# Making w_out the stationary operand of the MLP's second product, with sums in one PSUM tile per expert tile and earlier fetches for the first two experts

## The chip, the cores and the metric

The kernel runs on one core of one Trainium2 chip. The metric is the device time of one execution in microseconds (us). The kernel before was run three times: 5398.34, 5403.23 and 5403.87 us, median 5403.23. One further execution was profiled; it took 5409.9 us, of which the recorded span covers 5408.1 us, so 1.8 us lie outside the span.

## The reference, cut to what matters

Three stages on x of 8 x 3072 tokens with 256 features, all in float32.

```
scores = z @ z.T / S                     # z: 8 x 3072 x 64
x      = u * (relu(scores)**2 @ v)       # attention; u, v: 8 x 3072 x 256

e      = argmax(normalized(x) @ normalized(emb).T / tau)        # one of 8 experts
x      = gate * (relu(x @ w1[e]) @ w2[e])                       # 256 -> 1024 -> 256

h      = x @ w_in                                               # 256 -> 2048
x      = where(h > 0, h, exp(min(h, 0)) - 1) @ w_out            # 2048 -> 256
```

## The kernel before, in words

Matrix operands are split into a high and a low part, and a product is the sum of three: high by high, high by low, low by high. Each TensorE matmul has a stationary operand of 128x128 (loaded ahead of it) and a moving one of up to 512 columns, and adds to a PSUM tile.

The program is one list of 1166 steps. Step n issues on TensorE the first product of its own step (`h`, into a tile `pss`, two buffers) and the second product of the step two before (`acc`, into a tile `psa`, two buffers); between them ScalarE (ACT) and VectorE (DVE) make the hidden values and their high and low parts. The first 576 steps are attention: 48 chunks of 512 tokens, 12 steps each. Then come the units of the MoE and the MLP, laid out by a list: A is an expert's tile of 512 tokens (4 steps), B the 256-token remainder of an expert (2 steps), M the MLP on the tokens of an A (8 steps) and D the MLP on 512 remainder rows (8 steps). There are 41 A, 21 B, 41 M and 7 D. The first ones are A0 at step 576, A1 at 580, M0 at 584, A2 at 592, M1 at 596, A3 at 604, M2 at 608, A4 at 616; D0 begins at 1110 and the last, D6, at 1158. D6 has functions of its own (`l_h`, `l_acc`); `m_acc` is the second product of the 41 M and of the other six D, 47 units of 8 steps.

In `m_acc` the hidden values are stationary, 128 tokens at a time, and w_out moves: 8 matmuls of 512 columns (a high and a low half of w_out side by side) and 8 of 256 columns per step. The four token quarters stand in two PSUM tiles, `psa`, with the two sums (`wh` and `wl`) in 512 columns. In the last step of a unit ACT copies them out in four pieces (`o`, `o2`, line 1057 and 1058), and one step later `m_out` adds the two on DVE and scatters four blocks of 128 rows to the output with indirect DMAs.

Attention's second product is laid out the other way: v is stationary, the hidden values move, and the sums stand in one `psa` tile, features on partitions. `evac_ops` turns such a tile in 32x32 blocks on DVE (`tr`), writes it to DRAM in four pieces (`put`) and reads it back as rows (`get`).

Work beside the products is laid into steps: `at` puts it after step n's own instructions, `spread` and `pairs` deal it over a stretch of steps by given costs. Every engine and each of the two DMA queues (SP and POOL) works in the order of the program. POOL carries the indirect DMAs: scatters of token numbers by expert into `tok` (line 573, `sc` of `route_ops`; each waits until the one before it has landed), gathers of token numbers (`ids`), of token rows (`rows`) and of an expert's weights (`wst`) on line 779, and scatters of result rows to `out` on line 784. The tokens are routed in 24 groups, of which the first 22 end in attention; the last two are laid into the units. Each group has eight scatters of token numbers. `rows` are then put to DRAM (`xg`) and read back in the blocked layout by SP.

At the start `zero_dram` fills `tok` and the last four chunks of `xs` with zeros through SP. `slot` gives out SBUF from a ring of 48 tiles that all kinds share, in order of the program: an operation waits until the readers of what its slot held before are done.

Of the kernel before, what the change touches and what calls it, by code (L numbers as in the profile page):

```python
# [16 lines left out]
LAG = 2  # L17
# [10 lines left out]
def attn_moe_mlp(ctx, tc, zT, u, v, emb, tau, wp, w_in, w_out, out):  # L28
# [26 lines left out]
    xg = dr.tile([(NA + NB) * 512, D], F32, name="xg")  # L55
    tok = dr.tile([E * N, 1], I32, name="tok")
# [161 lines left out]
    def zero_dram():  # L218
# [6 lines left out]
        for C in range(NCH - 4, NCH):  # L225
            sp.dma_start(xs[C * 512:(C + 1) * 512, :].rearrange("(t p) d -> p t d", p=128),
                         zt.bitcast(F32).rearrange("p (t d) -> p t d", t=4))
# [171 lines left out]
    def att_acc(C, m):  # L399

        if m == 0:
            AC[C] = t_acc()
        hi, lo = HL.pop((C, m))
        vt = V[C // NC, m]
        for part in range(2):
            for dc in range(2):
                a = AC[C][:, dc]
                for j in range(2):
                    vh, vl = (vt[:, j, o + dc * 128:o + dc * 128 + 128] for o in (0, 256))
                    if part == 0:  # L410
                        mm(a, vh, hi[:, j], m == 0 == j, False)
                        mm(a, vl, hi[:, j], False, False)
                    else:
                        mm(a, vh, lo[:, j], False, m == CS - 1 and j == 1)

    def evac_ops(C):

        g, o = chunk_group[C]
        h = {}
        rows = xr[C * 512:(C + 1) * 512, :]  # L420

        def tr():
            h["t"] = slot("xt", F32, (16, 2, 32))
            vec.transpose(out=h["t"], in_=AC.pop(C).rearrange("p a (b r) -> p b a r", r=32))
# [6 lines left out]
        def get():  # L431
            X[C] = slot("x", F32, (4, 256))
            sp.dma_start(X[C], rows.rearrange("(t p) d -> p t d", p=128))
# [383 lines left out]
    def rows_ops(key):  # L817
# [9 lines left out]
        def gi(t):  # L827
            def fn():
                if t == 0:
                    IDS[key] = sb.tile([128, 4], I32, name="ids", tag="ids", bufs=6)  # L830
# [105 lines left out]
    PR = set()  # L936

# [44 lines left out]
    def l_acc(key, i):  # L982
# [15 lines left out]
        if last:  # L998
            if hf == 0:
                PS[key] = slot("o", F32, (4, 256)), None  # L1000
            o = PS[key][0][:, 2 * hf:2 * hf + 2]
            cp(o, a[:, :, 256:])
            tt(o, o, a[:, :, :256], ALU.add)
            for fn in m_out(key)[1 + 2 * hf:3 + 2 * hf]:
                fn()
# [28 lines left out]
    def m_acc(key, i):  # L1034
        if i == 0:
            AC[key] = [t_acc(), t_acc()]
        hi, lo = HL.pop((key, i))
        w = WO[i]
        last = i == NF2 // 2 - 1
        for qs in ((0, 1), (2, 3)) if last else ((0, 1, 2, 3),):  # L1040
            for part in range(2):
                for q in qs:
                    a = AC[key][q // 2][:, q % 2]
# [368 lines left out]
```

## Time and profile before

| | |
|---|---|
| median of three runs | 5403.23 us (5398.34 to 5403.87) |
| profiled execution | 5409.9 us |
| its span | 5408.1 us |
| mean granted TensorE clock | 0.996 |
| TensorE busy | 5363.7 us (99%) |
| VectorE busy | 4245.2 us (78%) |
| ScalarE busy | 4086.1 us (76%) |
| POOL busy | 1393.0 us (26%) |

The share of an engine is its busy time over the span. A busy TensorE includes matmuls that run at a lower granted clock and the modelled ends of matmuls, so the distance between starts tells more than the busy time: 512 columns at the full clock start 227 ns apart. In the rows of a timeline, consecutive instructions of one kind are joined (x8), the first number is the start, the second the time to the end of the last; the bracket holds the idle time before the instruction and what ended it.

### The profile page before, as it was taken

What the parts mean: (1) busy time and instruction counts of PE and PEld (TensorE: products, weight loads), DVE (VectorE), ACT (ScalarE), POOL (GpSimd) and SP (SyncE); (2) the same over time, 40 slices, a digit from 0 to 9 for tenths busy, and PEclk for the clock granted to TensorE, in tenths of its full rate; (3) what the DMA queues carried; (4) which work ended last, traced back from release to release, by engine and by line L of the source; (5) the groups of instructions that cost most, each with busy time, mean ns of one, the idle gap of its engine ahead of it and who ended that gap; (6) DMA issues with size and microseconds to landing.
All of it is one profiled execution on the core that took longest, in us unless ns stands there. A gap on an engine that the chain in (4) does not pass through costs nothing. (4 is left out here: it accounts for less than half of the span.)

```text
span 5408.1 us, 73322 instructions
## 1 busy us (share of the span) xinstructions
PE 5363.7 (99%) x26064; PEld 4531.1 (84%) x26064; DVE 4245.2 (78%) x7905; ACT 4086.1 (76%) x4764; POOL 1393.0 (26%) x1205
## 2 busy tenths in 40 slices
PE   9999999999999999999999999999999999999998
PEld 7888888888888887888888888888888888888887
DVE  8888888888888887887777777777777777777887
ACT  7989988898899985666666666666666666666786
POOL 0011101011111104323444444344544122231011
PEclk9999999999999999999999999999999999999999
DMA  3333333232323325112332323232323122221110
GB/s 111 86 79 86 79 86 84 73 90 75 86 81 76 83 58 178 57 52 87 92 100 86 103 89 98 88 106 89 100 84 110 45 68 67 67 67 36 20 24 20
DMA packets 465743, 428.17 MB, mean 79 GB/s; under 512 B 276380, under 2 KB 407199, under 8 KB 465376
## 3 DMA queue, kind: packets, MB, share of 16 engines
q1 hardware_dynamic: 388480, 216.86, 15.2%
q0 software_dynamic: 76896, 206.62, 12.2%
q8 instruction: 206, 3.38, 0.3%
q14 instruction: 161, 1.32, 0.1%
HBM read 293.72 MB, written 119.40 MB: 76 GB/s over the span
## 5 line engine op out<-in xcount | busy, mean ns | idle before, releaser
L104 PE MATMUL psa<-hi,v 128*128 128x512 f32 x4608 | 1143.8, 390 | 2.7 <-DVE hi L387 2.7
L104 PEld LDWEIGHTS psa<-hi,v 128*128 128x128 f32 x4608 | 865.1, 188 | 182.6 <-DVE hi L387 3.9
L83 DVE TENSOR_TENSOR lo<-r,hi 128x1024 fp32r<-128x1024 f32 x576 | 705.7, 1225 | 243.7 <-ACT hi L101 238.5
L104 PE MATMUL pss<-x2h,wi 128*128 128x512 f32 x2624 | 814.1, 391 | 0.0
L104 PE MATMUL psa<-wo,hi 128*128 128x512 f32 x3072 | 775.6, 390 | 0.6 <-DVE hi L1025 0.6
L366 ACT ACTIVATE r<-pss 128x1024 f32<-128x1024 f32 x576 | 591.2, 1026 | 208.4 <-PE pss L104 205.3
L93 DVE SCALAR_TENSOR_TENSOR y<-e,y 128x1024 f32<-128x1024 f32 x384 | 467.6, 1218 | 323.8 <-ACT e L1010 323.6
L957 ACT ACTIVATE e<-pss 128x1024 f32<-128x1024 f32 x376 | 386.5, 1028 | 393.0 <-PE pss L104 389.0
L104 PEld LDWEIGHTS psa<-wo,hi 128*128 128x128 f32 x3072 | 574.0, 188 | 117.4 <-DVE hi L1025 0.9
L371 ACT ACTIVATE r<-r 128x1024 f32<-128x1024 f32 x576 | 611.5, 1062 | 18.3
L573 POOL DMA_INDIRECT tok<-idt,pi x192 | 236.6, 1232 | 1505.3 <-DVE pi L552 859.7
L104 PE MATMUL psa<-lo,v 128*128 128x512 f32 x2304 | 616.7, 389 | 0.0
L95 DVE SCALAR_TENSOR_TENSOR junk<-x,en 128x256 f32<-128x256 f32 x1536 | 602.5, 419 | 0.0
L784 POOL DMA_INDIRECT out<-o,ids x192 | 201.8, 1051 | 1551.6 <-DVE o L83 508.3
L884 ACT ACTIVATE hi<-pss 128x1024 fp32r<-128x1024 f32 x206 | 211.8, 1028 | 495.3 <-PE pss L104 430.5
L104 PEld LDWEIGHTS pss<-x2h,wi 128*128 128x128 f32 x2624 | 476.5, 189 | 86.4
L104 PE MATMUL pss<-x2l,wi 128*128 128x512 f32 x1312 | 510.4, 389 | 0.0
L104 PEld LDWEIGHTS psa<-lo,v 128*128 128x128 f32 x2304 | 433.3, 188 | 90.2
L101 ACT ACTIVATE hi<-r 128x1024 fp32r<-128x1024 f32 x462 | 490.5, 1062 | 14.6
L83 DVE TENSOR_TENSOR y<-r,y 128x1024 f32<-128x1024 f32 x384 | 470.6, 1225 | 33.2 <-DVE y L93 0.5
L83 DVE TENSOR_TENSOR lo<-y,hi 128x1024 fp32r<-128x1024 f32 x384 | 470.8, 1226 | 30.5 <-DMA xg<-rows 8.9
L104 PEld LDWEIGHTS psa<-wo,lo 128*128 128x128 f32 x3072 | 429.5, 190 | 41.1 <-DVE lo L83 7.8
(160 smaller groups left out, 9935.7 us busy)
## 6 DMA issues: line engine op xcount, KB each, us to landing
vs<-v SPq DMA_DIRECT2D x48, 512.0 KB, 5.1
u<-u SPq DMA_DIRECT2D x48, 512.0 KB, 5.3
xr<-xt SPq DMA_DIRECT2D x192, 128.0 KB, 2.6
x<-xr SPq DMA_DIRECT2D x48, 512.0 KB, 4.4
xs<-x SPq DMA_DIRECT2D x48, 512.0 KB, 5.0
xg<-rows SPq DMA_DIRECT2D x41, 512.0 KB, 2.9
xt<-xg SPq DMA_DIRECT2D x164, 128.0 KB, 3.0
zz<-zT SPq DMA_DIRECT2D x46, 256.0 KB, 5.3
```

Source lines behind the costliest of these rows:

```text
L83: vec.tensor_tensor(out=o, in0=a, in1=b, op=op)
L93: vec.scalar_tensor_tensor(out=o, in0=a, scalar=s, in1=b, op0=op0, op1=op1)
L95: vec.scalar_tensor_tensor(out=o, in0=a, scalar=s, in1=b, op0=op0, op1=op1, accum_out=acc)
L101: act.activation(out=o, in_=a, func=AF.Copy)
L104: pe.matmul(o, lhsT=l, rhs=r, start=start, stop=stop, skip_group_check=True)
L366: act.activation(out=r, in_=p, func=AF.Relu, scale=1.0 / S)
L371: act.activation(out=r, in_=r, func=AF.Square)
L573: pool.indirect_dma_start(out=tok[:, :], out_offset=bass.IndirectOffsetOnAxis(ap=h["pi"][:, t:t + 1], axis=0), in_=K["idt"][:, gt:gt + 1], ...
L784: pool.indirect_dma_start(out=dst, out_offset=bass.IndirectOffsetOnAxis(ap=idx, axis=0), in_=src, in_offset=None, bounds_check=bound, oob_ ...
L884: act.activation(out=hi, in_=p, func=AF.Relu)
L957: act.activation(out=e, in_=p, func=AF.Relu, scale=-1.0)
```

## The change

Four edits.

1. The MLP's second product takes the layout of attention's: `vw_acc`, cut out of `att_acc`, serves both. w_out is stationary, the hidden values move: 12 matmuls of 512 columns per step into one `psa` tile. In the last step of a unit `out_ops` turns the tile on DVE, then SP writes it to a new DRAM tile `orow` in four pieces and reads it back as rows, and four scatters to the output follow at steps n+13 and n+14 of a unit that began at n. The ACT copies and the DVE addition of the 47 units go. The columns of w_out come permuted from the host, and `l_acc` of the last unit puts its features back in order as it copies, one quarter at a time.
2. The eight scatters of token numbers of a group are laid one a step, from the step on in which all eight stood.
3. The rows of A0 are gathered from step 556 on (before: 563), its weights from 560 (567); the rows of A1 from 562 (567).
4. `zero_dram` fills eight chunks of `xs` instead of four. The `ids` tiles get eight buffers instead of six.

The core of the diff:

```diff
@@ -53,6 +53,7 @@
+    orow = dr.tile([N, D], F32, name="orow")
...
@@ -222,7 +223,7 @@
             sp.dma_start(tv[a], zt[:, :E * N // 256])
-        for C in range(NCH - 4, NCH):
+        for C in range(NCH - 8, NCH):
             sp.dma_start(xs[C * 512:(C + 1) * 512, :].rearrange("(t p) d -> p t d", p=128),
                          zt.bitcast(F32).rearrange("p (t d) -> p t d", t=4))
...
@@ -396,32 +397,25 @@
-
-        if m == 0:
-            AC[C] = t_acc()
-        hi, lo = HL.pop((C, m))
-        vt = V[C // NC, m]
+    def vw_acc(a, w, hi, lo, first, last):
+
         for part in range(2):
             for dc in range(2):
-                a = AC[C][:, dc]
                 for j in range(2):
-                    vh, vl = (vt[:, j, o + dc * 128:o + dc * 128 + 128] for o in (0, 256))
+                    wh, wl = (w[:, j, o + dc * 128:o + dc * 128 + 128] for o in (0, 256))
                     if part == 0:
-                        mm(a, vh, hi[:, j], m == 0 == j, False)
-                        mm(a, vl, hi[:, j], False, False)
+                        mm(a[:, dc], wh, hi[:, j], first and j == 0, False)
+                        mm(a[:, dc], wl, hi[:, j], False, False)
                     else:
-                        mm(a, vh, lo[:, j], False, m == CS - 1 and j == 1)
-
-    def evac_ops(C):
-
-        g, o = chunk_group[C]
+                        mm(a[:, dc], wh, lo[:, j], False, last and j == 1)
+
+    def rows_by_dram(rows, acc, get_tile):
+
         h = {}
-        rows = xr[C * 512:(C + 1) * 512, :]
         def tr():
             h["t"] = slot("xt", F32, (16, 2, 32))
-            vec.transpose(out=h["t"], in_=AC.pop(C).rearrange("p a (b r) -> p b a r", r=32))
+            vec.transpose(out=h["t"], in_=acc().rearrange("p a (b r) -> p b a r", r=32))
         def put():
             for i in range(4):
@@ -429,8 +423,21 @@
                              h["t"][i * 32:(i + 1) * 32].rearrange("p b a c -> p b (a c)"))
         def get():
+            sp.dma_start(get_tile(), rows.rearrange("(t p) d -> p t d", p=128))
+        return tr, put, get
+
+    def att_acc(C, m):
+        if m == 0:
+            AC[C] = t_acc()
+        vw_acc(AC[C], V[C // NC, m], *HL.pop((C, m)), m == 0, m == CS - 1)
+
+    def evac_ops(C):
+
+        g, o = chunk_group[C]
+        def x_tile():
             X[C] = slot("x", F32, (4, 256))
-            sp.dma_start(X[C], rows.rearrange("(t p) d -> p t d", p=128))
+            return X[C]
+        tr, put, get = rows_by_dram(xr[C * 512:(C + 1) * 512, :], lambda: AC.pop(C), x_tile)
         def mul():
             if o == 0:
...
@@ -827,7 +834,7 @@
-                    IDS[key] = sb.tile([128, 4], I32, name="ids", tag="ids", bufs=6)
+                    IDS[key] = sb.tile([128, 4], I32, name="ids", tag="ids", bufs=8)
...
@@ -997,12 +1005,13 @@
         if last:
             if hf == 0:
-                PS[key] = slot("o", F32, (4, 256)), None
-            o = PS[key][0][:, 2 * hf:2 * hf + 2]
-            cp(o, a[:, :, 256:])
-            tt(o, o, a[:, :, :256], ALU.add)
-            for fn in m_out(key)[1 + 2 * hf:3 + 2 * hf]:
-                fn()
+                PS[key] = slot("o", F32, (4, 256))
+            for q in range(2):
+                o = PS[key][:, 2 * hf + q]
+                ov = o.rearrange("p (i b c) -> p b i c", i=4, b=2)
+                cp(ov, a[:, q, 256:].rearrange("p (b i c) -> p b i c", i=4, b=2))
+                tt(ov, ov, a[:, q, :256].rearrange("p (b i c) -> p b i c", i=4, b=2), ALU.add)
+                scatter(out[:, :], o, IDS[key][:, 2 * hf + q:2 * hf + q + 1], N - 1)
     def m_g(key, i):
         p, e, y = PS[key, i]
...
@@ -1033,48 +1042,31 @@
     def m_acc(key, i):
         if i == 0:
-            AC[key] = [t_acc(), t_acc()]
-        hi, lo = HL.pop((key, i))
-        w = WO[i]
-        last = i == NF2 // 2 - 1
-        for qs in ((0, 1), (2, 3)) if last else ((0, 1, 2, 3),):
-            for part in range(2):
-                for q in qs:
-                    a = AC[key][q // 2][:, q % 2]
-                    sl = slice(q * 128, q * 128 + 128)
-                    for j in range(2):
-                        st = last and j == 1
-                        if part == 0:
-                            mm(a, hi[:, j, sl], w[:, j], i == 0 and j == 0, st)
-                        else:
-                            mm(a[:, :256], lo[:, j, sl], w[:, j, :256], False, st)
-            if last:
-                q = qs[1]
-                if q == 1:
-                    PS[key] = slot("o", F32, (4, 256)), slot("o2", F32, (4, 256))
-                o, t = PS[key]
-                ap = AC[key][q // 2]
-                cp(t[:, q - 1:q + 1], ap[:, :, 256:])
-                cp(o[:, q - 1:q + 1], ap[:, :, :256])
-
-    def m_out(key):
-        def add():
-            o, t = PS[key]
-            tt(o, o, t, ALU.add)
+            AC[key] = t_acc()
+        vw_acc(AC[key], WO[i], *HL.pop((key, i)), i == 0, i == NF2 // 2 - 1)
+
+    def out_ops(key):
+
+        i = OUTS.setdefault(key, len(OUTS))
+        h = {}
+
+        def tile_():
+            h["o"] = slot("o", F32, (4, 256))
+            return h["o"]
         def sc(q):
             def fn():
                 ids = IDS["A", key[1]] if key[0] == "M" else IDS[key]
-                scatter(out[:, :], PS[key][0][:, q], ids[:, q:q + 1], N - 1)
-            return fn
-        return [add] + [sc(q) for q in range(4)]
+                scatter(out[:, :], h["o"][:, q], ids[:, q:q + 1], N - 1)
+            return fn
+        return rows_by_dram(orow[i * 512:(i + 1) * 512, :], lambda: AC.pop(key), tile_) + tuple(sc(q) for q in range(4))
     def d_prep(key):
         h = {}
         def ld():
             h["t"] = slot("xt", F32, (16, 2, 32))
-            IDS[key] = sb.tile([128, 4], I32, name="ids", tag="ids", bufs=6)
+            IDS[key] = sb.tile([128, 4], I32, name="ids", tag="ids", bufs=8)
             j = key[1]
             rows = dn[j * 512:(j + 1) * 512, :].rearrange("(b r) (a i c) -> i r b a c", r=32, a=2, i=4)
             for i in range(4):
...
@@ -1278,8 +1270,8 @@
         w += L
-        for s_ in sc:
-            at(w, s_, 1)
+        for i, s_ in enumerate(sc):
+            at(w + i, s_, 1)
         spread(gs, w, w + L, 0.2)
         route_end[g] = w
...
@@ -1314,12 +1306,15 @@
             wr = max(n - 9, lo_)
+            if un == units[0]:
+                w, wr = n - 16, n - 20
+                assert wr >= lo_
             if pv is not None and pv[0] == "B" == k:
                 assert False
             if pv is not None and pv[0] == "M" and prev[pv] is not None and prev[pv][0] in "AB":
                 wr = max(n - 16, lo_)
-            elif k == "A" and un[1] < 2:
-                wr = max(n - 13, lo_)
+            elif un == units[1]:
+                wr = n - 18
             for o in ro:
                 at(wr, o, 2)
             for o in wl:
...
@@ -1348,8 +1343,12 @@
             spread([tr], n - 4, n - 3, 1.25)
             pre[n - 2] += hl
         if k in "MD" and un != units[-1]:
-            w = n + nst[k] + LAG + (2 if k == "D" else 0)
-            spread(m_out(un), w, w + 2)
+            w = n + nst[k] + LAG - 1
+            tr, put, get, *sc = out_ops(un)
+            at(w, tr)
+            at(w + 1, put)
+            at(w + 2, get)
+            spread(sc, w + 4, w + 6)
     def emit(n, k):
         if 0 <= n < len(steps):
...
@@ -1380,8 +1379,7 @@
-    B, S, _ = v.shape
-    vp = v.reshape(B, S, 4, 2, 32).transpose(0, 1, 3, 2, 4).reshape(B, S, D)
+    vp, op = (t.reshape(-1, 4, 2, 32).transpose(0, 2, 1, 3).reshape(t.shape) for t in (v, w_out))
@@ -1390,7 +1388,7 @@
-        "w_in": c(w_in).view(np.int64), "w_out": c(w_out).view(np.int64),
+        "w_in": c(w_in).view(np.int64), "w_out": c(op).view(np.int64),
```

POOL's indirect DMAs around A0, in the kernel before: `zq<-zp` closes attention's own part, `tok` are the scatters of token numbers of group 21, `ids`, `rows` and `wst` the gathers of A0, of A1 and the ids of A2.

```order
L325 DMA zq<-zp 64x1024
L326 DMA zq<-zp 64x1024
L573 DMA tok<-idt,pi 196608x1 x8
L779 DMA ids<-tok,ixa 128x1 x4
L779 DMA rows<-xs,ids 128x256 x4
L779 DMA wst<-wp,wia 128x1024 x4
L779 DMA ids<-tok,ixa 128x1 x4
L779 DMA rows<-xs,ids 128x256 x4
L779 DMA wst<-wp,wia 128x1024 x4
```

The same place in the changed kernel, whose lines are numbered differently:

```order
L326 DMA zq<-zp 64x1024
L327 DMA zq<-zp 64x1024
L786 DMA ids<-tok,ixa 128x1 x4
L786 DMA rows<-xs,ids 128x256 x4
L580 DMA tok<-idt,pi 196608x1
L786 DMA wst<-wp,wia 128x1024 x4
L580 DMA tok<-idt,pi 196608x1 x2
L786 DMA ids<-tok,ixa 128x1 x4
L786 DMA rows<-xs,ids 128x256 x4
```

A0's ids and rows stand ahead of all eight scatters, its weights behind one of them, A1's ids and rows behind three; five more follow.

POOL's DMAs a little later, in the kernel before, from the conversion of the MLP's weights (`wi`, `wo`) on: the gathers behind the eight scatters are A3's.

```order
L1147 DMA wi<-wis 128x1024 x8
L1153 DMA wo<-wos 128x1024 x8
L779 DMA wst<-wp,wia 128x1024 x4
L573 DMA tok<-idt,pi 196608x1 x8
L779 DMA ids<-tok,ixa 128x1 x4
L779 DMA rows<-xs,ids 128x256 x4
```

And in the changed kernel:

```order
L1139 DMA wi<-wis 128x1024 x8
L1145 DMA wo<-wos 128x1024 x8
L786 DMA wst<-wp,wia 128x1024 x4
L580 DMA tok<-idt,pi 196608x1 x5
L786 DMA ids<-tok,ixa 128x1 x4
L786 DMA rows<-xs,ids 128x256 x4
L580 DMA tok<-idt,pi 196608x1 x3
L786 DMA wst<-wp,wia 128x1024 x4
```

A3's gathers stand behind five scatters instead of eight; the last three come after them.

DVE at the end of M0 (step 593) in the changed kernel: `lo<-pss,hi` belongs to an A step, `w<-wst,w` splits weights, `junk,dot<-x,en` are the dot products of the routing.

```order
L84 TENSOR_TENSOR y<-r,y 128x1024
L1034 CAST hi<-y 128x1024
L84 TENSOR_TENSOR lo<-y,hi 128x1024
L94 SCALAR_TENSOR_TENSOR lo<-pss,hi 128x1024
L84 TENSOR_TENSOR w<-wst,w 128x512 x3
L418 STREAM_TRANSPOSE xt<-psa 128x1024
```

Before, the same rows stand there without the last one; the addition `o<-o,o` of M0 came later, between the dot products of the next step. The turning of the PSUM tile is new at this place, with the dot products of the step behind it.

## Rows read from the trace of the kernel before

**Rows 1.** The page: busy time, share of the span and instructions of each engine.
```profile
PE 5363.7 (99%) x26064; PEld 4531.1 (84%) x26064; DVE 4245.2 (78%) x7905; ACT 4086.1 (76%) x4764; POOL 1393.0 (26%) x1205
```

**Rows 2.** Timeline of PE in one MLP step: start, us, engine, line, operation, tiles.
```profile
2334.00 0.63 PE L104 MATMUL pss<-x2h,wi 128*128 128x512 f32 x2
...
2336.75 1.98 PE L104 MATMUL psa<-wo,hi 128*128 128x512 f32 x8
2338.56 1.12 PE L104 MATMUL psa<-wo,lo 128*128 128x256 f32 x8
2339.51 0.63 PE L104 MATMUL pss<-xh,w 128*128 128x512 f32 x2
```

**Rows 3.** Timeline of PE: an expert step (two starts), and sixteen MLP steps.
```profile
2224.06 0.61 PE L104 MATMUL pss<-xh,w 128*128 128x512 f32 x2
2229.50 0.61 PE L104 MATMUL pss<-x2h,wi 128*128 128x512 f32 x2
...
5250.90 0.63 PE L104 MATMUL pss<-xh,wi 128*128 128x512 f32 x2
5339.18 0.40 PE L104 MATMUL pss<-xh,wi 128*128 128x256 f32 x2
```

**Rows 4.** Timeline of PE: the step starts on either side of three stalls.
```profile
2080.32 0.39 PE L104 MATMUL pss<-zp 128*128 128x512 f32 x1
2104.60 0.39 PE L104 MATMUL pss<-zp 128*128 128x512 f32 x1
...
2205.92 0.63 PE L104 MATMUL pss<-xh,w 128*128 128x512 f32 x2
...
2345.03 0.63 PE L104 MATMUL pss<-xh,w 128*128 128x512 f32 x2
2364.83 0.62 PE L104 MATMUL pss<-xh,w 128*128 128x512 f32 x2
```

**Rows 5.** Busy times in the first stall: stretch, then PE, PEld, DVE, ACT, POOL, PEclk, DMA.
```profile
2080.00:2104.00 24.00, 14.78 (x49) 11.05 (x48) 11.62 (x24) 14.04 (x21) 16.15 (x15) 0.72 0.70 210
```

**Rows 6.** Timelines of ACT and DVE: the three waits behind the stalls.
```profile
2085.87 0.63 ACT L101 ACTIVATE w<-wst 128x512 fp32r<-128x512 f32 x1 [8.48 <-DMA wst<-wp,wia]
...
2213.45 1.02 ACT L884 ACTIVATE hi<-pss 128x1024 fp32r<-128x1024 f32 x1 [11.48 <-DMA xg<-rows]
...
2353.43 1.23 DVE L83 TENSOR_TENSOR lo<-y,hi 128x1024 fp32r<-128x1024 f32 x1 [8.88 <-DMA xg<-rows]
```

**Rows 7.** Timeline of POOL: first scatter of eight, and first gather behind them, three times.
```profile
2032.34 1.05 POOL L573 DMA_INDIRECT tok<-idt,pi  x1 [49.92 <-DVE pi L552]
...
2068.97 1.10 POOL L779 DMA_INDIRECT ids<-tok,ixa  x1 [2.70 <-DMA tok<-idt,pi]
...
2156.27 1.14 POOL L573 DMA_INDIRECT tok<-idt,pi  x1 [0.30 <-DVE junk L95]
...
2197.18 1.04 POOL L779 DMA_INDIRECT ids<-tok,ixa  x1 [3.02 <-DMA tok<-idt,pi]
...
2302.22 1.63 POOL L573 DMA_INDIRECT tok<-idt,pi  x1 [0.30 <-issue]
...
2336.64 1.95 POOL L779 DMA_INDIRECT ids<-tok,ixa  x1 [2.39 <-DMA tok<-idt,pi]
```

**Rows 8.** Groups by line, engine and tile: busy us, mean ns, idle before.
```profile
L424 DVE STREAM_TRANSPOSE xt<-psa 128x1024 f32<-128x1024 f32 x48 | 60.0, 1249 | 81.3 <-PE psa L104 81.3
```

**Rows 9.** Timelines of ACT and DVE at the end of an MLP unit.
```profile
5172.46 1.09 ACT L101 ACTIVATE o<-psa 128x512 f32<-128x512 f32 x2 [0.35 <-PE psa L104]
5177.02 1.23 DVE L93 SCALAR_TENSOR_TENSOR y<-e,y 128x1024 f32<-128x1024 f32 x1 [3.59 <-ACT e L1010]
```

**Rows 10.** Timelines of SP's queue and ACT at the start.
```profile
9.72 6.79 SPq L226 DMA_DIRECT2D xs<-zt  x4
26.81 0.62 ACT L101 ACTIVATE v<-vs 128x512 fp32r<-128x512 f32 x1
```

**Rows 11.** The page, DMA issues: KB each and median us from issue to landing.
```profile
x<-xr SPq DMA_DIRECT2D x48, 512.0 KB, 4.4
```

More of the change, by code (lines that the diff above doesn't have):

```diff
@@ L397, in att_lo @@
         HL[C, m] = [hi, lo]
-    def att_acc(C, m):
-        if m == 0:
-            AC[C] = t_acc()
-        hi, lo = HL.pop((C, m))
-        vt = V[C // NC, m]
+    def vw_acc(a, w, hi, lo, first, last):
         for part in range(2):
             for dc in range(2):
-                a = AC[C][:, dc]
                 for j in range(2):
-                    vh, vl = (vt[:, j, o + dc * 128:o + dc * 128 + 128] for o in (0, 256))
+                    wh, wl = (w[:, j, o + dc * 128:o + dc * 128 + 128] for o in (0, 256))
                     if part == 0:
-                        mm(a, vh, hi[:, j], m == 0 == j, False)
-                        mm(a, vl, hi[:, j], False, False)
-                    else:
-                        mm(a, vh, lo[:, j], False, m == CS - 1 and j == 1)
-    def evac_ops(C):
-        g, o = chunk_group[C]
+                        mm(a[:, dc], wh, hi[:, j], first and j == 0, False)
+                        mm(a[:, dc], wl, hi[:, j], False, False)
+                    else:
+                        mm(a[:, dc], wh, lo[:, j], False, last and j == 1)
+    def rows_by_dram(rows, acc, get_tile):
         h = {}
-        rows = xr[C * 512:(C + 1) * 512, :]
         def tr():
             h["t"] = slot("xt", F32, (16, 2, 32))
-            vec.transpose(out=h["t"], in_=AC.pop(C).rearrange("p a (b r) -> p b a r", r=32))
+            vec.transpose(out=h["t"], in_=acc().rearrange("p a (b r) -> p b a r", r=32))
         def put():
@@ L936, in attn_moe_mlp @@
     PR = set()
+    OUTS = {}
     def m_r(key, i):
```

## The prediction

> **What bounds the kernel now.** The busy times come first: TensorE is busy 99% of the span, the next engine, VectorE, 78% [rows 1]. So the time falls only where TensorE's own work gets shorter or where it stops waiting, and what the other engines gain or lose counts only once it reaches TensorE. The second view is therefore TensorE's timeline, read from step start to step start. Two things are to be seen in it. The MLP's steps are a little longer than the experts' although both multiply the same number of columns: 2334.00 to 2339.51 is 5.51 us [rows 2], against 5.44 for an expert step, and 88.28 / 16 = 5.52 over sixteen steps of the remainder units [rows 3]. And in the whole program, behind the start, there are three places where it stands still for long [rows 4]. Three attention steps are 48 matmuls of 0.2265 us (eight of 512 columns take 2338.56 - 2336.75 = 1.81 us [rows 2]), 10.9 us; from 2080.32 to 2104.60 they take 24.28, so 13.4 are lost. Two unit steps are 5.51 + 5.44 = 10.95; they take 18.14 from 2205.92 to 2224.06, the latter start in [rows 3], and 19.80 from 2345.03 to 2364.83: 7.2 and 8.85 lost. Together 29.4 us.
>
> The third view, the timelines of ACT and DVE, says what ends these: the landing of A0's weights after 8.48 us of waiting, and twice the landing of `xg`, an expert's rows, after 11.48 and 8.88 us [rows 6]. The fourth, POOL's, says why that data is late: ahead of the gathers stand eight scatters of token numbers, each waiting for the one before it. Eight last 2068.97 - 2032.34 = 36.6 us, 40.9 and 34.4 us: 4.6, 5.1 and 4.3 each [rows 7].
>
> **The second product.** Before, a step of it is 8 matmuls of 512 columns and 8 of 256; now it is 12 of 512, and the number of columns is the same. The eight of 256 take 2339.51 - 2338.56 = 0.95 us, where four of 512 take half of 1.81 = 0.905 [rows 2]. By these starts a step gains 0.045 us. By the length of whole steps it gains more: the new step is made of 24 matmuls of 512 columns, as an expert step is, so it should last 5.44, a gain of 0.07 to 0.077 [rows 2, 3]. I take 0.072, since the whole step is what repeats and the short rows are read from two differences of ends. The steps are 47 units of 8, 376 in all (the last unit keeps its own function): **-27.1 us**, with ends of 0.045 x 376 = 17 and 0.077 x 376 = 29.
>
> The Trainium skill speaks against this, on the page "TensorE: Matmul & The Clock Gate", section "Back-to-back issue gap": an isolated matmul's gap at the full clock is its columns over 2.4 plus 2.5 ns. By that, four matmuls fewer are 10 ns a step, 3.8 us in all, and the sum would come out 23 us higher. This trace differs: 226 ns for 512 columns and 119 for 256 mean about 12 ns that do not shrink with the columns, so the rows set the term, and what the skill's rule would give stands among the rivals.
>
> **What replaces the copies.** At the end of each of the 47 units four ACT copies and a DVE addition go; a DVE turning of the PSUM tile comes, 1.25 us each, as in attention [rows 8]. It waits for TensorE's last matmul of the unit, and behind it in DVE's queue stands the next step's chain from `y` on, for which the product two steps on waits. In the present kernel the two double copies run from 5172.46, and DVE idles 3.59 us before its next `y`, because ACT's `e` comes behind the copies [rows 9]. With the copies gone ACT is some 2.2 us earlier (two such groups of 1.09), the turning takes 1.25 of the 3.59, and the chain still begins no later than before. So 0 at most units. At two of them, M0's end at step 593 and M2's at 617, other DVE work is laid into the same step (nine dot products; the plan's small operations), and the cover is thinner: I take +0.5 each, **+1.0 us**, ends 0 and 2.5 (two whole turnings). The writing to `orow`, the reading back, some 4.4 us for 512 KB as for attention's rows [rows 11], and the scatters lie on queues behind which nothing is due within several steps of 5.4 us; the rows of the next units are fetched through the same SP queue five steps ahead, 27 us. Price 0. The last unit keeps its form, with copies half as wide: 0.
>
> **The fetches.** Stall 1: A0's weights now stand behind one scatter instead of eight. Seven of them are 7 x 4.58 = 32 us; ACT, which began to wait at 2085.87 - 8.48 = 2077.4, would have them at about 2054. Gone with over 20 us to spare: -13.4. Stall 2: A3's gathers stand behind five scatters instead of eight, 3 x 5.1 = 15 us earlier, against 11.48 us that ACT waited: 3.8 to spare, -7.2. Stall 3: three scatters less, 3 x 4.3 = 12.9 us, against 8.88: 4.0 to spare, although four scatters of result rows now come among them, each some 1.05 us on POOL, as a scatter of token numbers [rows 7], if it need not wait: -8.85. **-29.4 us.** What is late next: in the first stall's 24 us ACT did 14.04 and DVE 11.62 us of work [rows 5], in which the three steps have only 10.9 without the stall. So up to 3.2 us may come back, if all of ACT's work of the stretch must be done in it; much can be done ahead, and I take **+1.4**. TensorE's granted clock was 0.72 in that stretch [rows 5]; as there will be no long pause, I let it be full, and this is in the 13.4 already.
>
> **The zeros.** Four more 512 KB writes at the start stand in SP's queue ahead of a chunk of v: the present four take 6.79 us, so up to 6.8 us later at a first use which is at 26.81 [rows 10]. The chunk is split some steps before TensorE uses it, and most of the delay is hidden: **+0.5**, ends 0 and 6.8.
>
> **The sum.** -27.1 - 29.4 + 1.0 + 1.4 + 0.5 = -53.6. From the profiled execution's 5409.9 that is 5356; this execution was 6.7 us above the median of the three runs, and from 5403.2 it is 5349.6. The scatters' landings vary (4.3 to 5.1 us in their means), so some of the 6.7 may lie in the stalls, which go; a forecast of 5351 lies near the lower sum.
>
> **The rivals.**
> One stall stays (B). A3's and A5's spare is only about 4 us and rests on scatters that land at their mean; DVE and ACT arrive at these places earlier than before, since the stall in front has gone. Then 7 to 9 us return: 5358, to 5368 with the smaller gain of the product. Chance 0.18.
> The fetches only change places (D): the data is early but something else holds it, SP's order or an SBUF slot of the ring, and the 29.4 us stay in other rows: 5349.6 + 29.4 = 5379. Against it: all three waits of [rows 6] end on a landing behind POOL's chain, none on a slot. Chance 0.06.
> Columns alone count (C): a step of as many columns takes as long, and of 27.1 us nothing comes: 5377. The 0.95 against 0.905 us [rows 2] speak against it. Chance 0.04. By the rule of the Trainium skill cited above, 3.8 us instead of none, it would be 5373.
> The turning holds TensorE (E), slower than before. In attention DVE stands 81.3 / 48 = 1.69 us before each turning, waiting for TensorE [rows 8]. If in the 47 units this wait came out on the other side, at the product two steps on, it would be 47 x 1.69 = 79 us: 5349.6 + 79 = 5429. It decides the sign from 53.6 / 47 = 1.14 us a unit. For it: the MLP's chain is longer than attention's (four DVE operations a step instead of the splitting alone). Against it: the 3.59 us of idle at this very place [rows 9]. Chance 0.05.
> The forecast (A): 0.67, its own range 5341 to 5358.
>
> **How the numbers follow.** Low end: the lowest of the three runs, 5398.3, less 56.5 for the two gains without any addition is 5342, two us lower with the gain of 0.077: 5340. High end: B with the smaller gain, 5368. C, D, E and a little of A and B lie outside, about 0.2. A measurement of this kernel tells 0.2%, 10.8 us, from no change: 5392.4 and 5414.0 are the borders. A to D are faster. E reaches from a partial hold, which may end within the borders, to slower. Faster 0.95, same 0.02, slower 0.03.
>
> **What would show it.** TensorE's MLP steps 5.44 us apart, with `psa<-hi,wo` and `psa<-lo,wo` of 512 columns at 227 ns: right; at 5.5: C. Step starts around A0, A2 and A4 without gaps over 1 us, and no wait of ACT or DVE on `wst` or `xg` that TensorE follows: right; else B or D, by the tile that is named. TensorE waiting on `lo` or `hi` behind `xt<-psa` at the ends of M and D units: E. ACT's copies to `o` gone but for the last unit's, the DVE addition too. The forecast as a whole is wrong if the steps are shorter and the gaps are gone, and the time still is not under 5370.

## The result, and the profile after

The changed kernel takes 5352.4 us (median of four, 5351.9 to 5352.9) against 5401.5 for the kernel before (median of four, 5398.3 to 5403.9): a ratio of 0.9907, 95% interval 0.9896 to 0.9919. The forecast was 5351, its range 5340 to 5368. The profiled execution took 5352.9 us, with a span of 5351.0 us; 57.1 us less than the span of before.

The page of the changed kernel, busy times as in [rows 1]:
```profile
PE 5325.6 (100%) x24560; PEld 4448.5 (83%) x24560; DVE 4246.9 (79%) x7907; ACT 3985.5 (74%) x4578; POOL 1412.8 (26%) x1205
```
TensorE issues 1504 matmuls less (376 steps by four), DVE does the same work, ACT 100 us less.

TensorE's timeline in an MLP step of the changed kernel, against [rows 2], and where its steps 625 and 1164 start:
```profile
5195.00 0.62 PE L105 MATMUL pss<-xh,wi 128*128 128x512 f32 x2
...
5197.72 1.98 PE L105 MATMUL psa<-hi,wo 128*128 128x512 f32 x8
5199.53 1.07 PE L105 MATMUL psa<-lo,wo 128*128 128x512 f32 x4
5200.44 0.62 PE L105 MATMUL pss<-xh,wi 128*128 128x512 f32 x2
...
2367.40 0.61 PE L105 MATMUL pss<-x2h,wi 128*128 128x512 f32 x2
5316.10 0.40 PE L105 MATMUL pss<-xh,wi 128*128 128x256 f32 x2
```
The step is 5.44 us, as an expert step is [rows 3]. Steps 625 to 1164 take 2948.70 us.

The stretch of the first stall in the changed kernel, in the columns of [rows 5], and POOL's timeline ahead of it, against [rows 7]:
```profile
2076.00:2100.00 24.00, 24.00 (x108) 19.88 (x107) 21.84 (x45) 22.48 (x34) 12.43 (x11) 1.00 0.53 162
```
```profile
1982.78 1.08 POOL L786 DMA_INDIRECT ids<-tok,ixa  x1 [0.30 <-issue]
...
2009.03 1.48 POOL L786 DMA_INDIRECT rows<-xs,ids  x1 [20.28 <-PE pss L105]
...
2032.42 1.01 POOL L580 DMA_INDIRECT tok<-idt,pi  x1 [16.91 <-DVE pi L559]
2033.73 1.11 POOL L786 DMA_INDIRECT wst<-wp,wia  x1 [0.30 <-issue]
```
TensorE is busy all of the 24 us, at a granted clock of 1.00 (the 2.4 GHz level), where the mean was 0.72 before. The gathers of A0's rows begin 67 us earlier than in the kernel before (2009.03 against 2075.84), those of its weights 47 us earlier (2033.73 against 2081.12).

Where the time went is best seen by stretches between step starts. The table is worked out from the first matmul of a step in each kernel's timeline; what else differs of a span lies before step 560 (up to 3 us) and behind step 1164 (up to 0.5).

| kernel | steps 560 to 584 | 584 to 600 | 600 to 625 | 625 to 1164 |
|---|---|---|---|---|
| before | 116.05 | 94.91 | 146.28 | 2975.71 |
| e12: before again | 115.49 | 94.44 | 143.98 | 2975.71 |
| e1: fetches alone | 102.65 | 87.78 | 137.49 | 2975.71 |
| e3: scatters spread alone | 112.87 | 87.78 | 137.49 | 2975.71 |
| e4: A0, A1 early alone | 120.28 | 87.78 | 144.28 | 2975.71 |
| e5: A0 early alone | 111.96 | 87.78 | 145.59 | 2975.71 |
| e2: product alone | 113.63 | 87.46 | 143.51 | 2948.70 |
| e11: change, not spread | 122.48 | 87.79 | 145.08 | 2948.70 |
| after | 102.65 | 87.50 | 136.75 | 2948.70 |

The first three columns hold one stall each, the second and third also 10 and 14 of the 376 steps with a second product of the MLP. The last holds no stall; what differs in it is the MLP's second product. The change takes 13.4, 7.4, 9.5 and 27.0 us from them.

### The profile page after: what moved, and what is told of

It is laid out like the page before. It is cut to its first block, busy times and chain, and to the rows that moved or that the text cites. A ratio compares the mean times of both kernels' runs of the same rounds, so it can differ in the third digit from the quotient of the medians.

```text
span 5351.0 us, 70583 instructions
## 1 busy us (share of the span) xinstructions
PE 5325.6 (100%) x24560; PEld 4448.5 (83%) x24560; DVE 4246.9 (79%) x7907; ACT 3985.5 (74%) x4578; POOL 1412.8 (26%) x1205
## 5 line engine op out<-in xcount | busy, mean ns | idle before, releaser
L105 PE MATMUL psa<-hi,wo 128*128 128x512 f32 x3008 | 743.0, 389 | 0.0
L105 PEld LDWEIGHTS psa<-hi,wo 128*128 128x128 f32 x3008 | 564.5, 188 | 116.9
L105 PEld LDWEIGHTS pss<-x2h,wi 128*128 128x128 f32 x2624 | 489.9, 188 | 99.4
L105 PE MATMUL pss<-zp 128*128 128x512 f32 x1152 | 449.3, 390 | 6.7 <-DVE zp L84 5.8
L791 POOL DMA_INDIRECT out<-o,ids x192 | 216.5, 1127 | 883.0 <-DMA o<-orow 477.4
```

Source lines behind the costliest of these rows:

```text
L105: pe.matmul(o, lhsT=l, rhs=r, start=start, stop=stop, skip_group_check=True)
L791: pool.indirect_dma_start(out=dst, out_offset=bass.IndirectOffsetOnAxis(ap=idx, axis=0), in_=src, in_offset=None, bounds_check=bound, oob_ ...
```

## The experiments

The kernel before ran beside these with medians of 5404.6 to 5405.8 us (e12: one run, 5404.0). The changed kernel's 5352.4 is that of the first comparison.

**e1, the fetches alone.** The kernel before with:
```diff
-        for s_ in sc:
-            at(w, s_, 1)
+        for i, s_ in enumerate(sc):
+            at(w + i, s_, 1)
...
+            if un == units[0]:
+                w, wr = n - 16, n - 20
...
-            elif k == "A" and un[1] < 2:
-                wr = max(n - 13, lo_)
+            elif un == units[1]:
+                wr = n - 18
```
and with eight chunks zeroed and eight `ids` buffers.

> The kernel before with the three edits of the fetches (scatters of token numbers one a step, A0 and A1 fetched earlier, eight chunks zeroed), and the old second product. Theory: the three stalls stand in POOL's order alone and do not need the new product, so all three go: in the profile 29.4 less at most 1.5, a span of about 5380, MLP steps still 5.51. In the timed runs the gain is 20 to 29 us: the profiled execution of before lay 8 us above the median of its timed runs and that of the changed kernel 0.5, so some of the stalls seem to be longer in that profile than in most runs; 20 to 22 says that all of that difference lies in them, 29 that none of it does. Rival (the stalls go only since the new product frees ACT and DVE of copies and additions): at least one of the three gaps, 7 to 13 us, stays.


Measured: 5381.1 us, 24.1 less, ratio 0.9955 (0.9941 to 0.9968). No stall is left. The profile's stalls of before, measured against e1, are 13.4 + 7.1 + 8.8 = 29.3 us; in the timed runs 24 of them were there to gain. The rival is out: the old second product, with its copies and additions, was still there.

**e2, the product alone.** The changed kernel without the edits shown under e1, and with:
```diff
-        for C in range(NCH - 8, NCH):
+        for C in range(NCH - 4, NCH):
```

> The changed kernel with the fetches and scatters where they stood before (eight scatters in one step, four chunks zeroed). Theory: MLP steps of 5.44 instead of 5.51 us, 27.1 us of gain by 376 steps, and the three stalls as before, 13, 7 and 9 us. Rival (the two gains share something): the shorter steps come sooner to the same late data, so the stalls grow by about what the steps before them save, 1 us and less, since only some ten MLP steps lie ahead of the last one; the gain would still be 26 to 27. If it is under 20, the bare starts of the matmuls (0.045 us a step, 17 us) were the right term.


Measured: 5376.8 us, 28.3 less, ratio 0.9947 (0.9933 to 0.9961). 2948.70 us from step 625 on, as in the changed kernel: 27.0 less than before. In its profile the second stall is gone, against what was expected, the other two are 11.0 and 6.8 (table, against the changed kernel). That execution was the fastest of the five, 8.2 us under their median, so the others may have had the stall. e1 and e2 together make 52.4 us; the whole change, against the same 5405.1, 52.7. So the two halves add up.

**e3, the scatters spread alone.** The first part of e1's diff.

> The kernel before with the scatters of token numbers one a step and nothing else. Four of A0's eight stand ahead of its ids and rows then, and all eight still ahead of its weights; five ahead of A3's gathers. Theory: the first stall stays at 10 to 13 us, the other two (7.2 and 8.9) go: 16 us less than before in the profile. Rival (A0's rows, not its weights, are what is late at the first stall): it goes too, or all but 1 or 2 us of it.


Measured: 5390.4 us, 14.8 less, ratio 0.9975 (0.9964 to 0.9985). The later two stalls are gone, the first stays at 10.2, as expected, and it ends on A0's weights, so the rival is out:
```profile
2087.54 0.63 ACT L101 ACTIVATE w<-wst 128x512 fp32r<-128x512 f32 x1 [10.55 <-DMA wst<-wp,wia]
```

**e4, the early fetch alone.** The rest of e1's diff (the lines of `units[0]` and `units[1]`, and eight chunks zeroed).

> The kernel before with A0 and A1 fetched earlier (and eight chunks zeroed), the eight scatters of a group still in one step. A0's four weight gathers stand between the first four scatters. Theory: the first stall goes, 13.4 us, the other two stay at 7 and 9 us or grow a little, since ACT and DVE come to them without the first pause. Rival (the three are one chain, in which the first pause makes the later ones): the other two change by several us.


Measured: 5404.2 us, ratio 1.0002 (0.9993 to 1.0011): nothing gained. The first stall is not gone but 17.6 us long; the second is gone, though it was expected to stay, and the third is 6.8. The timelines of SP's queue, POOL and DVE in e4, and what SP's queue waited for from 2040 to 2090 (us in total, times, longest):
```profile
2046.46 37.05 SPq L584 DMA_DIRECT2D xs<-x  x2
2083.57 0.50 SPq L843 DMA_DIRECT2D xg<-rows  x1
...
2066.48 1.97 POOL L573 DMA_INDIRECT tok<-idt,pi  x1 [3.65 <-DMA tok<-idt,pi]
...
2076.41 0.99 POOL L779 DMA_INDIRECT rows<-xs,ids  x1 [0.31 <-ACT r L371]
...
2080.32 1.00 POOL L779 DMA_INDIRECT rows<-xs,ids  x1 [0.30 <-issue]
...
2087.74 0.69 DVE L387 CAST hi<-r 128x1024 fp32r<-128x1024 f32 x1 [15.12 <-DMA xs<-x]
...
SPq L584 <- DMA rows<-xs,ids: 36.2, 2, 32.4
```
The second of SP's two writes of `xs` stands in the program behind A1's gather, which reads `xs` at rows known only at run time, and it waits for that gather. The gather comes through POOL last, at 2080, behind the eight scatters; the write follows, and DVE, which does not read `xs` but wants the SBUF slot of the tile being written, stands for 15 us. In the changed kernel the same write leaves 20 us earlier:
```profile
2046.80 16.89 SPq L591 DMA_DIRECT2D xs<-x  x2
2063.74 0.50 SPq L850 DMA_DIRECT2D xg<-rows  x1
```
Laying a gather earlier in the program without making way for it on POOL has moved the wait to another queue.

**e5, A0 alone early.** As e4, but A1's fetch where it was:
```diff
-            elif k == "A" and un[1] < 2:
+            elif un == units[1]:
                 wr = max(n - 13, lo_)
```


> The kernel before with A0 alone fetched earlier (and eight chunks zeroed); A1's rows stay where they were in the program, the eight scatters of a group in one step. In e4 SP's second write of xs, a DMA that A1's earlier gather from xs must precede, stood from 2046 to 2083 until that gather had come through POOL behind the eight scatters, and DVE waited 15 us for an SBUF slot behind it. Theory: with A1's gather behind that write in the program the write does not wait, and the first stall goes but for 0 to 2 us; the later two stay, 7 and 9 us in their longer form, 0 and 5 in their shorter. Time 5388 to 5396. Rival (A0's early fetch itself, or its weights between the scatters, holds the first stall): as e4, about 5404.


Measured: 5398.0 us, ratio 0.9990 (0.9981 to 0.9999). The timelines of SP's queue and DVE:
```profile
2047.13 7.49 SPq L584 DMA_DIRECT2D xs<-x  x2
...
2066.14 2.35 SPq L848 DMA_DIRECT2D xt<-xg  x4
...
2092.24 0.36 SPq L843 DMA_DIRECT2D xg<-rows  x1
...
2097.68 1.25 DVE L856 STREAM_TRANSPOSE xf<-xt 128x1024 f32<-128x1024 f32 x1 [9.33 <-DMA xg<-rows]
2110.86 1.24 DVE L856 STREAM_TRANSPOSE xf<-xt 128x1024 f32<-128x1024 f32 x1
```
The write of `xs` no longer waits, so e4's mechanism is right; but the stall is 9.3 us, not 0 to 2, and the time 2 us over the expected range. The turning that stands there for 9.33 us is A0's (A1's is the one at 2110.86). Its own data was read back from 2066.14 on, yet it starts only when A1's rows have been written to `xg`, which it does not read; in the trace it carries the semaphores of A1's four gathers and of that write. So it is a slot again: the turning gets the one that A1's rows hold, and these come late, behind the eight scatters. In these runs the first stall goes only with A0 early, A1 early and the scatters spread; A1 left late with the scatters spread was not run.

**e6, 256 columns.** In the changed kernel, for the MLP:
```diff
+                    for c in (slice(0, 256), slice(256, 512)):
-                        mm(a[:, dc], wh, hi[:, j], first and j == 0, False)
+                        mm(a[:, dc, c], wh, hi[:, j, c], first and j == 0, False)
...
```
and so for the other two products. This kernel leaves a part of the products out of its sums; the matmuls' number and size are as described.

> The changed kernel with each of the twelve matmuls of 512 columns of the MLP's second product in two of 256, same operands and sums (376 steps). Theory: a matmul costs some 12 to 13 ns whatever its columns, so twelve more are 0.15 to 0.16 us a step: steps of 5.59 to 5.60, 56 to 60 us slower, 5408 to 5413. Rival (columns over 2.4 plus 2.5 ns, the rule of the Trainium skill): 0.03 us a step, 11 us slower. Rival (columns alone count, and the gain of the change came from the layout in another way, such as fewer PSUM tiles): no change.


Measured: 5420.3 us, 67.9 more than the changed kernel and 8 to 12 more than the theory had. TensorE's timeline:
```profile
5250.68 2.08 PE L105 MATMUL psa<-hi,wo 128*128 128x256 f32 x16
5252.59 1.12 PE L105 MATMUL psa<-lo,wo 128*128 128x256 f32 x8
5253.55 0.63 PE L105 MATMUL pss<-xh,wi 128*128 128x512 f32 x2
...
5256.30 2.08 PE L105 MATMUL psa<-hi,wo 128*128 128x256 f32 x16
```
24 matmuls of 256 take 2.87 us where 12 of 512 take 2.72, 12.5 ns for each additional one. But the step is 5.62, 0.18 longer: the twelve matmuls of 512 behind them take 2.75 instead of 2.72 us. Both together are 15 ns for an additional matmul. Both rivals, 0 and 11 us, are out.

**e9, the old shapes in the new layout.** Only the product with the low part is cut in two:
```diff
-                        mm(a[:, dc], wh, lo[:, j], False, last and j == 1)
+                        for c in (slice(0, 256), slice(256, 512)):
+                            mm(a[:, dc, c], wh, lo[:, j, c], False, last and j == 1)
```

> The changed kernel with the four matmuls on the low part in eight of 256 columns: the shapes of the kernel before, 8 x 512 and 8 x 256 a step, in the new layout (w_out stationary, one PSUM tile, no copies). Theory: the gain of the product is the four matmuls less, nothing else of the layout. e6 gave 0.177 us a step for twelve more, 14.8 ns each; four more are 0.059, 22 us slower than the changed kernel, 5373 to 5376, against the 27 that the change gained; 5 us of the 27 would be the layout's. Rival (the layout, the two PSUM tiles or the order of the stationary operands, brings most of it): under 12 us slower. Rival (a matmul of 256 columns costs more beside low parts): the whole 27.


Measured: 5380.4 us, 27.9 more than the changed kernel, 0.7 from e1, which has the old layout. TensorE's timeline:
```profile
5221.25 0.63 PE L105 MATMUL pss<-xh,wi 128*128 128x512 f32 x2
...
5224.00 1.98 PE L105 MATMUL psa<-hi,wo 128*128 128x512 f32 x8
5225.81 1.11 PE L105 MATMUL psa<-lo,wo 128*128 128x256 f32 x8
5226.77 0.63 PE L105 MATMUL pss<-xh,wi 128*128 128x512 f32 x2
```
5.52 us, as before: 0.05 in the eight matmuls of 256, 0.03 in the first product behind them. The theory's 22 us were too low: e6's mean of 15 ns spreads the 0.03 us over twelve matmuls, and here there are four. From step 625 to 1164 e9 takes 2974.26 us: of the 27.0 us that the change gains there, 25.6 are the four matmuls, and at most 1.5 are left for all else in the layout (no copies, one PSUM tile, rows through DRAM).

**e7 and e8, more turnings.** The line that turns the PSUM tile of an MLP unit, done three and five times:
```diff
+            for _ in range(1 + more):
-            vec.transpose(out=h["t"], in_=acc().rearrange("p a (b r) -> p b a r", r=32))
+                vec.transpose(out=h["t"], in_=src)
```


> The changed kernel with the turning of each of the 47 units' PSUM tile done three times on DVE instead of once (2.5 us more at each unit's end). Theory: TensorE does not wait for the turning; what is behind it in DVE's queue has 2.9 us to spare at an expert step and 3.5 at an MLP step (from DVE's end to TensorE's use of what it made). So nothing at nearly all units, 2.5 us each at the two where other DVE work fills the step: 3 to 8 us slower in all. Rival (the turning lies on the path, as the slower case of the prediction has it): 47 x 2.5 = 118 us slower.

> As the last, with the turning done five times (5.0 us more). Theory: the spare 2.9 us are exceeded by 2.1 at the 40 units that an expert step follows, the 3.5 us by 1.5 at the six remainder units: 70 to 100 us slower. Rival (on the path from the first): 235 us. Rival (DVE's work at the ends of units has room without limit): under 10 us.


Measured: 5367.6 us, 15.2 more, and 5509.7, 157 more. Both theories were too low; the turning is not on the path from the first (118 and 235 us), nor has DVE room without limit (under 10). In e7 some 8.5 us stand at the ends of M0 to M3, and 0.19 us at each of some 34 later units. DVE and TensorE at one of these, and the wait at M2's end:
```profile
3513.45 3.82 DVE L420 STREAM_TRANSPOSE xt<-psa 128x1024 f32<-128x1024 f32 x3 [1.42 <-PE psa L105]
...
3517.11 0.39 PE L105 MATMUL psa<-lo,w 128*128 128x512 f32 x1
3517.42 0.70 PE L105 MATMUL psa<-hi,w 128*128 128x512 f32 x2
...
2340.08 0.73 PE L105 MATMUL pss<-xh,w 128*128 128x512 f32 x2 [2.66 <-DVE lo L94]
```
and in e8:
```profile
3577.29 6.38 DVE L420 STREAM_TRANSPOSE xt<-psa 128x1024 f32<-128x1024 f32 x5 [1.41 <-PE psa L105]
...
3583.82 0.70 PE L105 MATMUL psa<-hi,w 128*128 128x512 f32 x2 [2.49 <-DVE xt L420]
```
The next expert unit's second product stops at its third pair, until the turning has ended, in e8 at 38 units. An expert unit takes two PSUM tiles of the two there are; the second is the one being turned. It had 2.5 - 0.2 = 2.3 us to spare in the changed kernel, less than the 2.9 us of the chain in DVE's queue that the expectation went by. Of e8's 157 us, 119 stand in the steps with this wait; 21 in the steps behind them, at some of which matmuls run at a lower clock for a while (granted 0.87 from 2618.0 to 2623.8, behind such a pause); and 17 at the other nine units, where TensorE waits for DVE's `hi` behind the turning, 1.8 each.

**e10, one PSUM tile per expert unit.** e8 and:
```diff
-            AC[key] = [t_acc()[:, 0] for _ in range(2)]
+            t = t_acc()
+            AC[key] = [t[:, dc] for dc in range(2)]
```


> e8 (the turning five times) with one more edit: an expert unit keeps its two sums in one PSUM tile of two banks instead of in one bank each of two tiles. In e8 TensorE stood 2.49 us at 35 units until the turning ended, at the third pair of the expert's second product, which is where it first writes its second tile; with two buffers that is the tile that the MLP unit ahead of it has just filled. Theory: that buffer is what holds TensorE, with 2.3 us to spare in the changed kernel (e7: 2.5 us more cost 0.19 a unit). With one tile per expert unit it is not needed, the waits on the turning go, and what stays is the chain behind it in DVE's queue, with 2.9 us to spare: 60 to 115 us slower than the changed kernel instead of 157. Rival (it is DVE's queue alone that holds TensorE): 157 as before.


Measured: 5590.4 us, 238 more than the changed kernel. TensorE's timeline:
```profile
3614.63 1.02 PE L105 MATMUL pss<-xh,w 128*128 128x512 f32 x2 [2.24 <-DVE lo L94]
...
3633.22 0.73 PE L105 MATMUL psa<-hi,w 128*128 128x512 f32 x2 [1.41 <-DVE x2l L84]
```
No matmul waits for the turning any more, as expected. In their place 38 units wait for DVE's `lo` behind the turning, 2.24 us at most of them; that costs 99 us in these steps and 45 in the steps behind, again with matmuls at a lower clock (granted 0.82 from 2633 to 2639). The other nine units cost 18, about as in e8. And expert units now wait 1.4 to 1.8 us at their last step, 77 us in all with the slower matmuls after it; the edit itself brought that, since the two halves of the sum now share a tile. So the buffer is the first limit, with 2.3 us to spare, but DVE's queue is next with 5.0 - 2.4 = 2.6, not 2.9. Without the new wait the sum is 162 us, about e8's 157: the theory's 60 to 115 is wrong, and taking the buffer away gains nothing at this length.

**e11, the change without the spreading.** The changed kernel with:
```diff
-        for i, s_ in enumerate(sc):
-            at(w + i, s_, 1)
+        for s_ in sc:
+            at(w, s_, 1)
```

> The changed kernel with the eight scatters of a group in one step again, everything else kept (A0 and A1 fetched earlier, new product). Theory from e3 and e4: the earlier fetch gains nothing without the spreading, since A1's gather stands behind eight scatters and SP's second write of xs waits for it; so this should be e4 (5404) less the product's 28: 5374 to 5380, about e2. Rival (the parts add up, 13 us for the earlier fetch): 5364.


Measured: 5381.8 us (5378.5 to 5385.7), 29.4 more than the changed kernel, 5.0 more than e2 and 2 over the expected range. The first stall is longer than before, 19.8 us:
```profile
2093.78 1.65 PE L105 MATMUL psa<-hi,v 128*128 128x512 f32 x3 [15.27 <-DVE hi L388]
```
The earlier fetch is worth something only with the spreading, 24.1 against 14.8 us for the spreading alone. Alone it gains nothing that the runs tell from their spread: 0.9 us in e4, and e11 is not faster than e2, whose runs lie between 5368.6 and 5379.3.

**e12, the kernel before again.**

> The kernel before, unchanged, profiled once more. The question is why its profiled execution took 5409.9 us and its other runs 5397 to 5410, while kernels without the three stalls (e1, e3, the changed kernel) stay within 2 us. Theory: the eight chained scatters land sooner or later from run to run, and the stalls take up the difference: the steps outside of the three stalls agree with the first profile to within 2 us, and the difference of the two spans lies in the stalls. Rival: the differences are spread over the whole span (clock or memory).


Measured: a span of 5403.1 us, 5.0 less than the first profile. The stretches without a stall behind the third step agree to 0.01 us; 0.6, 0.5 and 2.3 us of the difference lie in the stalls, and 1.7 before the third step. So two thirds of it are the stalls and the rest the start. The three chains of eight scatters are 0.4, 1.3 and 0.3 us shorter than in the first profile, from first to last start; that does not account for the third stall, so how the scatters land is not all that varies. The kernels whose stalls are all gone stay within 1.1 us (the changed kernel) and 1.6 us (e1) from run to run, e3, which keeps only the first stall, within 1.7; those that keep the third within 4 to 13.

## Why the prediction was right, point by point

**The product, -27.1.** From step 584 on the changed kernel takes 28.0 us less than e1 (0.3 + 0.7 + 27.0 in the table). The ends of M0 and M2, below, have cost 1.0 there, so the product itself brought 29.1, or 0.077 us for each of the 376 steps: 27.3 in these steps and 1.8 in the steps right behind the units. The choice of the step's length over the starts of the short matmuls was right, but of its two values, 0.072 and 0.077, the larger was the right one. e9 and the timelines say where the length and the starts differ: behind a run of short matmuls the first product takes 0.03 us more. Columns alone (C) is out: e6 shows 12.5 ns beside the columns within the run and 15 in all. The Trainium skill's rule for an isolated matmul, 2.5 ns beside the columns ("TensorE: Matmul & The Clock Gate", "Back-to-back issue gap"), does not hold for this stream by the same figures.

**The fetches, -29.4.** In the profiles 29.3. What landed late, and behind what, was right: A3's and A5's rows, mended by the spreading (e3), and A0's weights, mended by order. How this reached TensorE was right for the first stall alone. In the other two rows of [rows 6], ACT's `hi<-pss` and DVE's `lo<-y,hi` do not read `xg`; in the trace they carry the semaphores of the four gathers of rows and of their write to `xg`. They wait for the SBUF slot that A3's and A5's rows hold until they are written out. Earlier gathers free the slot earlier, so the sum came out all the same. What was wrong too is the working for the first stall, which counted seven scatters less ahead of A0's weights and stopped there. By that, the early fetch alone would gain 13 us; it gains nothing (e4, e11), because A1's gather binds SP's write of `xs` and, without that (e5), A1's own late rows hold a slot. The prediction gave against rival D that no wait ends on a slot; two of its three do, and those of e4 and e5 as well. D's mechanism is real, and the spreading keeps it off: in the changed kernel the write of `xs` leaves at 2063.7 instead of 2083.6. The spare time of 3.8 and 4.0 us was enough; B did not come.

**What comes back, +2.9.** Entry of the experts: 1.4 forecast, none measured; ACT did 22.48 and DVE 21.84 us of work in the 24 us that TensorE was busy throughout. Unit ends: 1.0 forecast, 0.5 at each of M0's and M2's; the two steps there take 5.73 and 5.61 us and 5.88 and 5.57 instead of 5.44 each, 0.5 and 0.6 us more in all, as forecast. The row at M2:
```profile
2334.63 0.74 PE L105 MATMUL pss<-xh,w 128*128 128x512 f32 x2 [0.27 <-DVE lo L94]
```
The zeros: 0.5 forecast; from the third step to the 560th the four kernels with four chunks take 2024.0 us, those with eight 2024.1 (the changed kernel's profile) to 2026.0, so up to 2 us, of which the changed kernel's profile happens to show 0.1.

**The sum.** -53.6 against the profiled execution, measured -57.1. Of the 3.5 between, 2.0 are the product and 1.8 the allowances for the experts' entry and the zeros. Against the median it was measured at -49.1 in the first comparison and -52.7 beside e1 to e4, since the stalls of a median run are smaller than the profile's. The forecast lay between the sums from the two bases, nearer to the lower one; the measured time is 1.4 us above it. That the point came out so close is in part luck, since misses cancelled: the product and the allowances came out nearly 4 us better than summed, and the stalls were taken from a run in which they were long (29.4; e1 gained 24.1 in the timed runs).

**The turning (E).** DVE waits 67.7 us before the 47 turnings:
```profile
L418 DVE STREAM_TRANSPOSE xt<-psa x47: 1249/1249/1251, 2197.8 to 5293.5; 128x1024 f32<-128x1024 f32 x47
...
  PE psa L105: 67.7, 47
```
That is 1.44 each, and TensorE loses none of it but at M0's and M2's ends, as forecast. But the cover that was named, DVE's idle time, is not what decides first: the PSUM tile that the next expert unit needs does, with 2.3 us to spare (e7, e8), and DVE's queue next, with 2.6 (e10). Neither part of the prediction looked at who takes that tile next.

**What stays open.** The second stall is also gone in the profiles of e2, e4, e5 and e11, in which POOL's order at that place is the old one. There A3's first gather of token numbers starts 31.4 to 34.1 us after TensorE's step 584; in the two profiles that have the stall it is 40.7 and 40.6, and the stall 7.1 and 6.7. So it turns on that distance, not on POOL's order alone. In e4, e5 and e11 the chain of eight scatters begins 7.7 us before step 584 (before: 0.2); in the kernel before, POOL has stood 5.90 us at a gather of weights ahead of it, for the landing of a `xg<-rows`. In e2 the chain is shorter, 28.7 us from first to last start against 36.3. Why it landed faster there stays open. Each of these kernels was profiled once, so whether the stall is gone in their other executions is not shown.

## What to carry to other kernels

Price a matmul change by the length of a whole repeated step that already has the new shapes, not by the starts of the changed matmuls. An instruction laid earlier in the program is early only if its queue lets it be: list what stands ahead of it there, and also what must now stand behind it on other queues (here a write that a gather with unknown rows binds). When an instruction waits for a DMA whose data it does not read, ask which buffer it is being given. When a reader of a PSUM tile grows longer, look up who takes that buffer next; here that was a nearer limit than the reading engine's own queue, by 0.3 us.

## What the runs showed that was not expected

The stretch of 539 steps behind the stalls agrees to 0.01 us between six profiles of kernels with the old product, while the stalls behind eight chained scatters differ by up to 2.3 us between two profiles of one kernel; here the kernels that keep such stalls late in the program are those whose times spread. A run of matmuls of 256 columns costs 12.5 ns for each more than 512 columns would need, and a further 0.03 us in the matmuls of 512 columns that follow.
